# Retention attention into a low-rank mixer: half chunks of q and k loaded as rows of four tokens, k scaled in place of v in batch 0, one column tile for U^T x, and V loaded first as 32 rows

## The chip, the core and the metric

The kernel runs as one program on one core of a Trainium2 chip. The metric is the device time of one execution in microseconds (us); smaller is better. Five runs of the kernel before the change are known, and one further execution was profiled.

## What is computed

```python
def _attn_ref(q, k, v):                       # q, k, v: 8 x 8 x 576 x 64, float32
    scores = scale * np.matmul(q, k.transpose(0, 1, 3, 2))
    gamma = 1.0 - 2.0 ** (-5.0 - np.arange(H))
    rel = pos[:, None] - pos[None, :]
    Dmat = np.where(rel >= 0, gamma[:, None, None] ** rel[None], 0.0)
    return np.matmul(scores * Dmat[None], v)

def _moe_ref(x, U, V, w_ch1, w_ch2):          # x: 8 x 576 x 512
    xt = x.transpose(0, 2, 1)
    h = xt @ U @ V                            # U: 576 x 32, V: 32 x 576
    u = x + h.transpose(0, 2, 1)
    ch = np.maximum(u @ w_ch1, 0.0) @ w_ch2   # 512 x 2048, 2048 x 512
    return u + ch
```

The heads' outputs of a batch, side by side, are x. A decay factor gamma^(i-j) is split into a factor of the query's position and a factor of the key's position, so that a scaling of rows does the decay.

## The kernel before

**Tiles.** A batch has 576 tokens, four chunks of 128 and a half chunk of 64. Batches go in pairs: chunks 0 to 3 belong to the even batch, 5 to 8 to the odd one, and chunk 4 (`XC`) holds the last 64 tokens of the even batch in partitions 0 to 63 and the first 64 tokens of the odd batch in partitions 64 to 127. `kA qA vA` are the half-chunk loads of batch 0, `kB qB vB` those of batch 1.

**Per chunk.** q, k and v come in as float32, are cast to bfloat16 (`qkv`), and q and k are transposed (`qkT`). TensorE makes the scores of a chunk (`SC`), VectorE masks them (`ret`), TensorE multiplies them by v (`RV`) and adds q times the running state (`QS`); the state is the sum of k^T v over earlier chunks (`ST`). The result x of a batch is multiplied by U (`MA`, into `a_sb`, 32 rows of results for a part of the tokens), and `a_sb` by V gives h; u = x + h.

**Mixer.** Tokens are taken in groups of four chunks (g = 0 to 8). A group runs 16 blocks of Y1 (u @ w1, Relu on ScalarE) and four rows of Y2 (y @ w2), 864 ns of TensorE work each piece. The first group needs batch 0 finished and the first weights; from then on TensorE has mixer work to run, and the attention of later batches is put between it.

**Batches 0 and 1** are loaded differently from the rest. q comes in rows of four tokens (`load_q4`, 1-KB rows), k and v in rows of two tokens (`load_pair`, 512-byte rows); the half chunks come token by token (`load(..., early=True)`, 256-byte rows into 64 partitions). In `load_pair` the argument `scaled` says which of k (1) and v (2) is multiplied by the key's decay factor `vs2`: that one is a TENSOR_TENSOR on POOL (or DVE), the other a plain cast on ACT (or POOL or DVE).

**Order.** A planner (`Plan`) gives every operation a duration, a priority and dependencies, and writes out one static order for each engine. All loads go through SP's queue; their order in batches 0 and 1 is the list `line`. DMA durations in the plan are constants in the code. While TensorE has nothing to do before the first Y1, the program puts multiplications by zero there (`zeros`, rows `ps_big_t<-zer`).

**Where the change falls.** In the first 24 us: setup of constants (`consts_a`: L275 to L322), the casts of q (L378) and its evictions (L416, L419), casts of k and v (L521, L523), scalings (L526), transposes of k (L566) and evictions (L575, L577), masks (L713, L857), x (L757, L759, L932), `MA` and `a_sb` (L962), the copy of V (L1173, L1177), the first u transposed (`build`, L1041 and L1043), the first w1 casts (L1197), and Y1. All matmuls that are not transposes have line L326. V is loaded by one DMA that repeats its 32 rows four times, 128 partitions in all, since the four chunks' terms of `MA` land in four column tiles of 32 rows.

## Time and profile before

| | us |
|---|---|
| five runs, median | 338.34 |
| five runs, lowest and highest | 336.23, 339.85 |
| the profiled execution, its own time | 336.47 |
| its span, first to last instruction | 334.3 |
| first Y1 matmul starts (from the span's start) | 24.31 |
| last DVE addition starts | 330.41 |

| engine | busy us | share of the span |
|---|---|---|
| PE (TensorE matmul) | 325.6 | 97% |
| PEld (weight load, beside PE) | 160.8 | 48% |
| DVE (VectorE) | 150.3 | 45% |
| ACT (ScalarE) | 134.9 | 40% |
| POOL (GpSimd) | 84.9 | 25% |

All times of the profile are counted from the start of the span. In a line of the timeline the columns are start, duration, engine, source line, operation, output<-inputs, shapes, and how many instructions were merged; in brackets stands the idle time before it and what ended that. "SPq" lines are DMA issues by SP. The duration of a matmul includes its passage through the array, so consecutive matmuls overlap; a 128x512 one lasts 379 ns and its successor starts 216 ns after it. The granted TensorE clock was 0.998 of full speed.

### The profile page before, as it was taken

Reading aid. Unit: us, or ns where it says so; the run is one execution under the profiler, and the core shown is the slowest. Engines: PE = TensorE matmul, PEld = TensorE weight load, DVE = VectorE, ACT = ScalarE, POOL = GpSimd, SP = SyncE. Lnnn points to the kernel's source line nnn. Section 1 sums busy time; section 2 is a strip of 40 time slices with the busy share of each in tenths; the row PEclk is TensorE's granted clock in tenths of the full one; section 3 lists DMA queues with packets and bytes.
Section 4 is the critical chain, followed back from the end, with each engine's and each line's share of the span. In section 5 each row is a group of like instructions: output and inputs, shape, how many; then the busy total and the mean of one; then the engine's idle time right before and its main releaser. Section 6 shows DMA issues by size and latency. Waiting matters only on the chain.

```text
span 334.3 us, 6464 instructions
## 1 busy us (share of the span) xinstructions
PE 325.6 (97%) x2656; PEld 160.8 (48%) x2656; DVE 150.3 (45%) x238; ACT 134.9 (40%) x240; POOL 84.9 (25%) x116
## 2 busy tenths in 40 slices
PE   8989989999999999999999999999999999999995
PEld 3554445555545544554454455444544444444442
DVE  5852275786654537654476538533633020020011
ACT  4656554478303550265114521364035206404600
POOL 7657446521331222131132112200100010010010
PEclk9999999999999999999999999999999999999999
DMA  8999999999999999999999989913110320011012
GB/s 238 228 286 377 296 248 299 274 231 182 194 248 214 232 182 209 229 238 198 192 241 221 193 178 227 225 35 49 63 65 16 71 89 31 0 65 63 0 52 75
DMA packets 145169, 56.44 MB, mean 169 GB/s; under 512 B 128244, under 2 KB 138484, under 8 KB 145140
## 3 DMA queue, kind: packets, MB, share of 16 engines
q1 hardware_dynamic: 142420, 47.12, 68.5%
q0 software_dynamic: 2720, 8.92, 7.7%
q8 instruction: 21, 0.34, 0.4%
q14 instruction: 8, 0.07, 0.1%
HBM read 37.14 MB, written 9.44 MB: 139 GB/s over the span
## 4 chain that ended last, share of the span: by engine, by line
PE 91%; DMA 5%; POOL 1%; DVE 1%; ACT 1%; SPq 0%; issue 0%; DVEq 0%
PE ps_big_t L326 77%; PE ps_s L326 5%; PE ps_o L326 5%; PE ps_sc L326 3%; DMA st_st<-in_k_dram 3%; DMA vst<-in_moe_V_dram 3%; PE ps_big_t L566 1%; PE ps_sc L401 1%; DVE ret_t L713 0%; SPq L1156 0%; ACT qkT_t L575 0%; POOL w_sb L1197 0%; DVE o_sb L1127 0%; POOL VV L1173 0%; POOL VV L1177 0%
## 5 line engine op out<-in xcount | busy, mean ns | idle before, releaser
L326 PE MATMUL ps_big_t<-uT_t,w_sb 128*128 128x512 bf16 x576 | 133.7, 379 | 0.5 <-POOL w_sb L1197 0.5
L326 PE MATMUL ps_big_t<-w_sb,y_t 128*128 128x512 bf16 x576 | 133.1, 379 | 0.0
L1060 ACT ACTIVATE y_t<-ps_big_t 128x512 bf16<-128x512 f32 x144 | 85.8, 597 | 93.9 <-PE ps_big_t L326 93.7
L326 PEld LDWEIGHTS <-w_sb 128*128 128x128 bf16 x576 | 53.9, 98 | 62.1 <-POOL w_sb L1197 1.0
L326 PEld LDWEIGHTS <-y_t 128*128 128x128 bf16 x576 | 53.7, 98 | 60.7 <-issue 0.5
L1127 DVE TENSOR_TENSOR o_sb<-ps_big_t,u_t 128x512 f32<-128x512 f32 x36 | 24.7, 690 | 87.7 <-PE ps_big_t L326 87.5
L1134 POOL DMA_DIRECT2D out_dram<-o_sb x34 | 19.4, 570 | 161.4 <-DVE o_sb L1127 161.2
L472 POOL TENSOR_TENSOR qkv_t<-st_st,vscale 128x512 bf16<-128x512 f32 (+1 forms) x28 | 29.4, 1050 | 57.5 <-DMA st_st<-in_v_dram 46.3
L857 DVE TENSOR_TENSOR ret_t<-ps_sc,tri 128x1024 bf16<-128x1024 f32 x24 | 29.3, 1221 | 20.0 <-PE ps_sc L326 19.8
L798 ACT ACTIVATE s_sb<-ps_s 128x512 bf16<-128x512 f32 x22 | 13.1, 596 | 56.5 <-PE ps_s L326 56.4
L923 DVE TENSOR_TENSOR x_t<-ps_o,qscale 128x512 bf16<-128x512 f32 x27 | 18.6, 689 | 16.2 <-PE ps_o L326 16.1
L991 DVE TENSOR_TENSOR u_t<-ps_s,x_t 128x512 bf16<-128x512 f32 x20 | 13.8, 690 | 21.2 <-PE ps_s L326 21.1
L326 PEld LDWEIGHTS <-qkT_t 64*128 64x128 bf16 (+3 forms) x612 | 15.4, 99 | 11.2 <-issue 8.2
L326 PEld LDWEIGHTS <-ret_t 128*128 128x128 bf16 (+2 forms) x384 | 12.7, 99 | 7.3 <-issue 1.3
L468 DVE CAST qkv_t<-st_st 128x512 bf16<-128x512 f32 x27 | 13.0, 482 | 3.4 <-DMA st_st<-in_k_dram 3.4
L468 DVE CAST qkv_t<-q_st 128x512 bf16<-128x512 f32 x27 | 13.4, 497 | 2.3 <-DMA q_st<-in_q_dram 2.2
L326 PE MATMUL ps_sc<-qkT_t 64*128 64x128 bf16 (+2 forms) x336 | 13.5, 215 | 0.5 <-DVE ret_t L857 0.4
L326 PE MATMUL ps_o<-qkv_t,ret_t 128*128 128x64 bf16 (+2 forms) x344 | 13.2, 193 | 0.0
L326 PE MATMUL ps_s<-qkv_t 64*64 64x64 bf16 (+3 forms) x200 | 12.4, 207 | 0.3 <-ACT s_sb L675 0.3
L326 PEld LDWEIGHTS <-qkv_t 64*64 64x64 bf16 (+3 forms) x232 | 9.7, 104 | 6.1 <-issue 2.6
L991 DVE TENSOR_TENSOR u_t<-ps_o,x_t 128x512 bf16<-128x512 f32 x16 | 10.9, 684 | 3.4 <-PE ps_o L326 3.3
L575 ACT ACTIVATE qkT_t<-ps_big_t 128x512 bf16<-128x512 bf16 (+1 forms) x21 | 10.9, 555 | 2.0 <-PE ps_big_t L566 1.7
(101 smaller groups left out, 178.6 us busy)
## 6 DMA issues: line engine op xcount, KB each, us to landing
out_dram<-o_sb POOLq DMA_DIRECT2D x34, 256.0 KB, 3.2
st_st<-in_k_dram SPq DMA_DIRECT2D x24, 256.0 KB, 4.8
q_st<-in_q_dram SPq DMA_DIRECT2D x24, 256.0 KB, 4.5
st_st<-in_v_dram SPq DMA_DIRECT2D x24, 256.0 KB, 4.9
y_t<-in_moe_w_ch_dram SPq DMA_DIRECT2D x10, 512.0 KB, 9.9
wst_t<-in_moe_w_ch_dram SPq DMA_DIRECT2D x6, 512.0 KB, 7.5
st_st<-in_k_dram SPq DMA_DIRECT2D x4, 512.0 KB, 8.5
st_st<-in_v_dram SPq DMA_DIRECT2D x4, 512.0 KB, 7.8
```

The costliest lines, as they stand in the source:

```text
L326: nc.tensor.matmul(*a, skip_group_check=True, **kw)
L401: tps[a].append(nc.tensor.transpose(pst[:, hp // 2, r, hp % 2, :], t[:, 0, 2 * hp:2 * hp + 2, :].rearrange("p h d -> p (h d)"), ident,))
L468: nc.vector.tensor_copy(**args)
L472: eng.tensor_tensor(out=qkv[slot(*qk)][rows, 2, :, :], in0=at(2)[rows], in1=vscale[rows, c, :, None].to_broadcast([rows.stop - rows.start, ...
L575: nc.scalar.activation(func=AF.Copy, **args)
L798: nc.scalar.activation(out=s_sb[slot(*sk)], in_=ps_s.rearrange("p (a b) -> p a b", b=P), func=AF.Copy)
L857: nc.vector.tensor_tensor(out=ret[slot(*rk)][rows, hl, :, 0:n], in0=bank(hl.start)[rows, None, :, 0:n] if apart else ps_sc[rows, hl, :, 0: ...
L923: nc.vector.tensor_tensor(out=xs[slot(*xk)][rows].rearrange("p hp hl d -> p hl hp d"), in0=po[rows, :, 0:NHP * D].rearrange("p hl (hp d) - ...
L991: nc.vector.tensor_tensor(out=us[slot(*uk)].rearrange("p (hp hl d) -> p hp hl d", hl=2, d=D), in0=bank().rearrange("p (hp hl d) -> p hp hl ...
L1060: nc.scalar.activation(out=y1s[slot(*yk)][:, f, :], in_=ps_big[slot(*bk)], func=AF.Relu)
L1127: nc.vector.tensor_tensor(out=osb[slot(*ok)], in0=ps_big[slot(*bk)], in1=osb[slot(*ok)] if n else us[slot(*uk)], op=ALU.add)
L1134: eng.dma_start(out=out_flat[row:row + P, :], in_=osb[slot(*ok)])
```

## The change

It does these things. (1) `kA`, `qA` and `qB` are loaded in rows of four tokens of one head, 1 KB, 128 partitions by 256 values; `xqs` holds the decay factors for this layout (they need two POOL iotas, two selects and some DVE and ACT operations in `consts_a`); a new `t_x` sorts and transposes them by eight 64x64 matmuls against columns of the identity in place of four transposes. (2) In batch 0 both chunk pairs scale k and cast v (`scaled=1`). (3) The terms of `MA` of batch 0 all go to column tile 0 and add up there; `a_sb[0]` is zeroed in the setup and only 32 rows of it are written. (4) V comes first as 32 rows, VV is zeroed whole in the setup; the other 96 rows come late (`lv2`), then all 128 rows are cast by POOL (`Vr`) and copied (`V2`). (5) The order of loads, some planned durations (`DMA_LAT` 1700 to 2100 among them) and the place of `XC`'s transposes and scores in the plan are others, and the planner writes out another order for all engines.

```diff
-    DMA_LAT = 1700.0
+    DMA_LAT = 2100.0
...
+        nc.gpsimd.iota(xsel[:, 1, :], pattern=[[-HALF, H]], base=0, channel_multiplier=0, ...)
+        for b in range(2):
+            nc.gpsimd.iota(xqs[:, b, :], pattern=[[1, 4]], base=HALF if b else 4 * P, channel_multiplier=4, ...)
         for h in range(H):
             nc.vector.memset(lngt[:, :, h], lng[h])
+        nc.vector.tensor_copy(out=xsel[:, 0, :], in_=lngt[:, 0, :])
+        nc.vector.tensor_tensor(out=xsel[:, 1, :], in0=xsel[:, 1, :], in1=lngt[:, 0, :], op=ALU.mult)
...
-        nc.vector.memset(VV[:, S:S + HALF], 0.0)
+        for m, base in ((1, 0), (-1, 15)):
+            nc.gpsimd.affine_select(out=xsel, in_=xsel, pattern=[[0, 2], [-16 * m, H]], compare_op=ALU.is_ge,
+                                    fill=0.0, base=base, channel_multiplier=m)
+        nc.vector.tensor_reduce(out=xln, in_=xsel, axis=mybir.AxisListType.X, op=ALU.add)
+        nc.scalar.activation(out=xqs, in_=xqs, func=AF.Exp, bias=xln[:, 1:2], scale=xln[:, 0:1])
+        nc.vector.memset(VV, 0.0)
+        nc.vector.memset(a_sb[0], 0.0)
...
+    def t_x(j, b, prio):
...
+        def fn(e):
+            for r in range(4):
+                for hl in range(2):
+                    mm(pst()[HALF * hl:HALF * hl + HALF, r, :], xflat(j, b)[:, D * r:D * r + D],
+                       ident.rearrange("p (hp hl a) -> p hp hl a", hl=2, a=16)[:, :, hl, :], start=True, stop=True)
+        o = pl.op("PE", 300.0, fn, [st["kq"[j < 1], kb], ld["id"]], prio, acq=[bk])
+        def ev(e):
+            args = dict(
+                out=qkT[slot("qkT", (0, XC))][:, j * NHP:(j + 1) * NHP, rows].rearrange("p h (a r) -> p r h a", r=4),
+                in_=pst().rearrange("p r (h a) -> p r h a", a=16))
...
+        def four(j):
+            return b is not None and j == 0 or b == 0 and j == 1
...
+                if four(j):
+                    _, bb, t0 = pts[0]
+                    sent.append(nc.sync.dma_start(
+                        out=flat(j), in_=dram[bb, :, t0:t0 + HALF, :].rearrange("h (a r) d -> h a (r d)", r=4)))
+                    return
...
+            if four(0):
+                eng.tensor_tensor(
+                    out=xflat(0, b).rearrange("p (r d) -> p r d", d=D),
+                    in0=flat(0).rearrange("p (r d) -> p r d", d=D),
+                    in1=xqs[:, b, :, None].to_broadcast([P, 4, D]), op=ALU.mult)
...
-        terms = [(UU[:, 6 * par + i, :], c0 + i, 32 * i, every) for i in range(4)]
+        one = p == 0 and par == 0
+        terms = [(UU[:, 6 * par + i, :], c0 + i, 0 if one else 32 * i, every) for i in range(4)]
...
-            out=a_sb[par], in_=bank(), func=AF.Copy), [o], prio, acq=[(f"a{par}", p)], rel=[pak])
+            out=a_sb[par][0:R] if one else a_sb[par], in_=bank()[0:R] if one else bank(), func=AF.Copy), ...)
...
-            nc.sync.dma_start(out=vst, in_=moe_V[None, :, :].to_broadcast([4, R, S]))
+            nc.sync.dma_start(out=vst[0:R, :], in_=moe_V)
...
+        ld["lv2"] = DMA(500.0, 700.0, lambda e: nc.sync.dma_start(
+            out=vst[R:P, :], in_=moe_V[None, :, :].to_broadcast([3, R, S])), prio=-999.0)
...
+        ld["V"] = pl.op("ACT", 680.0, vcast(slice(0, R)), [ld["lv"]], -935.0,
+                        alt=[("DVE", 600.0), ("POOL", 700.0)])
+        ld["Vr"] = pl.op("POOL", 700.0, vcast(slice(0, P)), [ld["lv2"], ld["V"]], -150.0)
         ld["V2"] = pl.op("POOL", 600.0, lambda e: gp.tensor_copy(
-            out=VV[:, S + HALF:NV], in_=VV[:, 0:S]), [ld["V"]], -150.0)
+            out=VV[:, S + HALF:NV], in_=VV[:, 0:S]), [ld["Vr"]], -149.0)
...
-            load_pair(0, i, base + 20 * i, scaled=(2, 2)[i])
+            load_pair(0, i, base + 20 * i, scaled=1)
...
-    line = [...("k0 k2 v0 kA qA v2 vA lu lv w0 w1" + " " + "w2 w3 w4 w5 w6 w7 w8 w9 q4 w10 w11 kB k5 qB vB v5 k7 w12 w13 w14 w15 lub v7").split()]
+    line = [...("kA k0 k2 v0 qA vA v2 lu lv w0 w1" + " " + "w2 w3 w4 w5 w6 q4 w7 w8 w9 w10 w11 k5 kB qB vB v5 k7 w12 w13 lub w14 w15 v7 lv2").split()]
```

## The prediction

> **What bounds the kernel now.** I read the page first, then TensorE's busy time by stages, the chain of waits, and the timeline of the first 25 us.
>
> ```profile
> PE 325.6 (97%) x2656; PEld 160.8 (48%) x2656; DVE 150.3 (45%) x238; ACT 134.9 (40%) x240; POOL 84.9 (25%) x116
> ```
>
> TensorE is the bound. The stages (start:end, span, then busy us of each engine, at the end clock, DMA share and GB/s) say where it is not:
>
> ```profile
> 16.00:22.00 6.00, 5.56 (x138) 4.24 (x138) 2.42 (x5) 3.39 (x7) 2.34 (x4) 1.00 1.01 230
> 22.00:24.30 2.30, 1.24 (x5) 0.38 (x4) 1.01 (x2) 1.19 (x2) 2.20 (x4) 1.00 1.05 385
> 24.30:38.00 13.70, 13.69 (x64) 6.23 (x65) 2.86 (x5) 8.14 (x14) 9.36 (x9) 1.00 1.06 373
> 38.00:50.00 12.00, 11.06 (x102) 5.65 (x101) 8.44 (x15) 6.11 (x13) 5.74 (x6) 1.00 1.09 236
> 50.00:66.00 16.00, 15.19 (x255) 9.24 (x255) 10.65 (x14) 7.36 (x13) 10.37 (x13) 1.00 1.08 284
> 66.00:330.00 264.00, 264.00 (x1897) 127.47 (x1895) 112.68 (x170) 99.25 (x171) 43.97 (x57) 1.00 0.71 143
> ```
>
> From 66 to 330 us TensorE never idles, so nothing there can gain. What can move is the start of Y1 at 24.31 (before it TensorE partly multiplies zeros, so "busy" says little) and 0.94 + 0.81 = 1.75 us of idling between 38 and 66, where batch 1 is worked in. The timeline says what Y1 waits for:
>
> ```profile
> 21.17 0.60 ACT L962 ACTIVATE a_sb<-ps_big_t 128x512 bf16<-128x512 f32 x1 [0.46 <-PE ps_big_t L326]
> 21.87 0.67 POOL L1173 CAST VV<-vst 128x576 bf16<-128x576 f32 x1 [2.69 <-DMA vst<-in_moe_V_dram]
> 22.59 0.59 PE L326 MATMUL ps_big_t<-VV,a_sb 128*128 128x512 bf16 x2 [0.74 <-POOL VV L1173]
> 23.21 2.12 POOL L1197 CAST w_sb<-wst_t 128x1024 bf16<-128x1024 f32 x2
> 23.29 0.69 DVE L1043 CAST uT_t<-ps_big_t 128x512 bf16<-128x512 f32 x1 [3.33 <-PE ps_big_t L326]
> 24.31 2.76 PE L326 MATMUL ps_big_t<-uT_t,w_sb 128*128 128x512 bf16 x12 [0.48 <-POOL w_sb L1197]
> ```
>
> `a_sb` is done at 21.77, but V arrives late and costs TensorE 22.59 - 21.82 = 0.77 us; POOL then copies V a second time, so the first w1 cast ends at 24.25 instead of before uT at 23.98, another 0.28. Two lines of the chain show the load, and the first row above its price: 6 us at 230 GB/s, against 385 just after, with DMA fully busy in both.
>
> ```profile
> 13.39 8.43 DMA vst<-in_moe_V_dram
> 42.25 8.52 DMA st_st<-in_k_dram
> ```
>
> **The change, part by part, against the profiled 336.47 us** (span 334.3, 2.2 around it; the median, 338.34, lies 1.87 higher, and I carry differences over).
>
> *V in 32 rows.* 72 KB go in place of 288, the weights follow without the slow stretch, and the second copy leaves the place ahead of w1. V is then wanted only at a_sb's end: -0.77 and -0.28, -1.05 in all if a_sb comes at 21.77. Does it?
>
> *The setup.* These rows set when q's casts start:
>
> ```profile
> 2.65 0.09 DVE L311 MEMSET VV<- 128x32 uint32 x1
> 3.01 0.27 DVE L313 MEMSET sx<- 128x256 uint32 x1
> 3.08 0.87 POOL L318 TENSOR_SCALAR_AFFINE_SELECT tri<-tri 64x256 bf16<-64x256 bf16 x2
> 4.78 3.08 POOL L378 TENSOR_TENSOR qkv_t<-q_st,qs 128x256 bf16<-128x256 f32 x4 [0.84 <-DMA q_st<-in_q_dram]
> ```
>
> Zeroing 608 words of VV instead of 32 costs DVE 0.46 (a line through 0.09 for 32 and 0.27 for 256), a_sb 0.27, and the small operations for `xqs`, one of which waits for POOL's new iota, some 0.9. tri's memset stands behind all these, so it ends at 4.64 and not 3.01, POOL's two selects at 5.55, and POOL's four q casts start at 5.6, not 4.78: +0.8, no longer hidden behind the q load. (The program also puts ACT's 1.28 us table load behind a DVE operation; it ends near 4.3, under cover of 5.25, when DVE is through.)
>
> *k scaled.* POOL: casts to 8.7, kA (half of a 0.61 cast) to 9.0, then k0's two tokens by multiplication, 1.04 each; one row where DVE multiplied at the same time took 1.55, and DVE now does (its evictions end at 10.5), so 11.5. Before, POOL and ACT cast them side by side by 9.28. The first mask goes from 10.62 to 11.5 + 0.85 = 12.35, +1.7. Four masks follow at 1.21, the third ends at 15.98, and RV of the first pair, which reuses its bank, goes from 14.98 to 16.3. What is won at the other end: v2 needs only a plain cast (0.61) behind its arrival, where scaling ended at 16.92. Its arrival was 15.3 (POOL's 0.50 wait for it ended there); I keep 15.3 to 16.0, so 15.9 to 16.6. TensorE gets there at 17.2. From there, in its order: the states 0.75, scores of the half chunk 0.12, the first U term 0.35: RV of the second pair at 18.4, before 18.04.
>
> *One column tile.* Before, four U terms in four column tiles took 0.32 until the next instruction; now each takes 0.216 alone. One runs ahead of RV, three between transposes that must run anyway: +0.5 of work, of which about 0.4 fits in the 0.35 and 0.19 gaps in which TensorE waited for x. I take +0.12. So a_sb ends at 21.77 + 0.36 + 0.12 = 22.25, V's product starts at 22.3, Y1 (1.44 later, 22.59 to 24.03) at 23.74: **-0.57**. Bounds: -1.4 if POOL's multiplications don't slow each other and the setup hides; +0.8 if the U cast, now wanted at 17.7 (it ran at 18.88, POOL being busy until then), holds TensorE, with RV, both later products and MA queued behind it.
>
> *1-KB rows.* In the DMA view, 256-byte rows ran at 228 GB/s (window 10 to 12 us), 1-KB rows at 353 (4 to 6 us): 128 KB in 0.57 and 0.37 us, so -0.2 each for kA and qA, 0 if the rows don't matter. kA now stands ahead of k0, so k0, first cast at 7.98 before, is 0.37 to 0.57 later, near 8.5, and POOL is free for it only at 9.0: no term on the path. Were POOL free, k0's delay would count in full.
>
> The Trainium skill, "DMA: Bandwidth & Descriptors", section "Why a DMA increments its semaphore by 16 and not by 1", says a DMA uses the largest number of engines up to 16 that divides the slowest dimension of both its sides. That speaks against this part: kA and qA have 8 heads outermost, so 8 engines each, and the 96 spare rows of V a 3. It agrees with V's 4 copies crawling at 230 GB/s, though no view here counts engines. By it kA would gain nothing (0.7 us on half the engines, an estimate) and the spare rows would crawl as long as V did; the sum above stays, since POOL is later than k0 either way.
>
> *Later.* From 16 to 22 us DMA moved 1.38 MB where 385 GB/s moves 2.3: 2.4 us lost, plus 0.6 for the 216 KB that wait: weights, k and v of batch 1 come about 3 us earlier, TensorE 0.57. Of the 1.75 us idle, what hangs on loads (the second line of the chain above, k landing at 50.77, idles TensorE 0.5) goes; waits for masks and evictions stay: **-0.5**, bounds -1.75 and +1, the order being another. qB's four extra matmuls and the rest: +0.1. The spare rows of V: 0, hidden as long as they land before 64; the copy is wanted at 65.77.
>
> Sum: -0.57 - 0.5 + 0.1 = -0.97: 335.5 in a profiled execution, 337.4 on the median. A measurement of this kernel tells about 1% (3.4 us) from no change; this is 0.3%.
>
> **The rivals.**
>
> *Everything arrives early.* Setup hides, Y1 starts at 22.9 (-1.4), and batch 1's idling goes whole (-1.75): 338.34 - 3.1 = 335.2. For it: DMA 24 to 38 us runs at 373 GB/s, so a lead is kept. Against it: the masks in batch 1 (1.2 us each on DVE) stay.
>
> *The setup and the scaled k eat the gain.* POOL is on the path from 5.6 to 12.5; if each multiplication takes 1.55 and the U cast is late too, Y1 starts at 24.9 and batch 1 gains nothing: +0.6, 338.9. For it: the 1.55 row; against: TensorE then has only real work left and fewer zeros to push.
>
> *The spare rows of V collide with batch 2 (the other side).* They follow v7, whose scaling waited until 58.3, and batch 2's k and q queue behind.
>
> ```profile
> 58.32 1.04 POOL L526 TENSOR_TENSOR qkv_t<-st_st,vs 128x512 bf16<-128x512 f32 x1 [0.57 <-DMA st_st<-in_v_dram]
> 63.58 0.52 DVE L468 CAST qkv_t<-q_st 128x512 bf16<-128x512 f32 x1
> 65.77 0.71 PE L326 MATMUL ps_sc<-VV,a_sb 128*128 128x128 bf16 x4
> ```
>
> With 3 us of lead, v7 lands at 55.3; if the rows then take V's 8.43, they land at 63.7, two casts put V's copy at 65.1, and q of batch 2's second chunk (63.5 before) comes at 63.5 - 3 + 8.4 = 68.9. Its cast stands on DVE ahead of uT's eviction, so Y1 of group 1 goes from 67.3 to about 71.5: +4.2 - 0.5, 342.0. It decides once the rows land later than about 64; against it, 5 us or less after v7 costs nothing.
>
> **How the numbers follow.** Forecast 0.60, early arrivals 0.12, gain eaten 0.19, collision 0.09. The likeliest is 337.4; the range takes in the eaten gain and most of the early case, with run medians moving some 0.5: 335.0 to 339.6. Faster by over 1% (below 335.0) needs the best of the early case: 0.10. Slower by over 1% (above 341.7) needs the collision: 0.08. Within 1%: 0.82.
>
> **What would show it.** V's product starts right behind a_sb, Y1 at 23.2 to 24.3; POOL's first q cast near 5.6; first mask near 12.3; no wait of TensorE for VV or w1 before Y1; 66 to 330 us still full. I am wrong if Y1 starts before 22.8 or after 24.8, or TensorE idles over 3 us between 38 and 75.

## The result, and the profile after

The changed kernel took 340.97 us (median of 23 runs, 337.83 to 342.74). The kernel before, run beside it, took 338.1 (median of 42 runs: 41 from 336.1 to 342.6 and one at 420.2). Runs over 1.5% above the fastest of their kernel, such as that one, count as a slower state of the chip and are left out of the ratios. The ratio is 1.0072, with a 95% interval of 1.0048 to 1.0096: slower by 0.7%, where 0.3% faster was forecast. That is still within the 1% that the prediction called no change, but the time lies outside its range of 335.0 to 339.6. The profiled execution took 340.39, with a span of 338.6, 4.3 us more than before.

On the page, the busy times of the engines are much as they were; nothing here says where 4.3 us went:

```profile
PE 328.3 (97%) x2664; PEld 160.5 (47%) x2664; DVE 151.0 (45%) x242; ACT 135.8 (40%) x241; POOL 85.1 (25%) x122
```

TensorE's busy time by stages does (the same stages as the prediction's; the last three columns are clock, DMA share and GB/s):

```profile
16.00:22.00 6.00, 5.84 (x188) 4.49 (x188) 4.50 (x6) 4.21 (x8) 3.79 (x6) 1.00 0.77 221
38.00:50.00 12.00, 10.11 (x90) 4.93 (x87) 4.18 (x9) 6.71 (x15) 5.71 (x7) 1.00 1.16 256
50.00:66.00 16.00, 15.68 (x251) 8.67 (x250) 11.04 (x15) 6.38 (x11) 10.77 (x14) 1.00 0.94 243
66.00:330.00 264.00, 263.06 (x1903) 127.07 (x1904) 112.00 (x171) 101.20 (x174) 44.78 (x58) 1.00 0.74 144
```

The first row is the one to look at. V no longer crawls there, and yet DMA moved 221 GB/s, no more than before's 230. What changed is the share: 0.77 where before had 1.01, so some of the 16 engines had nothing to do for part of the time. This row alone doesn't say why: a second profile of the same kernel has 0.89 at 253 GB/s there, and a profile with all loads on 16 engines but one engine late from the start (c1 again, below) has 0.77 as well. TensorE's busy time, the first number behind the span of a stage, says that 38 to 50 us idles TensorE 1.89 us (before: 0.94), and 66 to 330 us 0.94 (before: 0). With Y1, which starts 1.65 later, the idling from 24.3 us on (2.22 + 0.94, against 1.76) makes 3.05 of the 4.3. The other 1.25 stands in no wait that a view shows.

The timeline of the changed kernel, with the rows that answer to the prediction's:

```profile
10.27 3.49 POOL L594 TENSOR_TENSOR qkv_t<-st_st,vs 128x512 bf16<-128x512 f32 x3 [0.83 <-DMA st_st<-in_k_dram]
13.22 1.23 DVE L781 TENSOR_TENSOR ret_t<-ps_o,tri 128x1024 bf16<-128x1024 f32 x1 [0.36 <-PE ps_o L342]
18.38 0.61 POOL L591 CAST qkv_t<-st_st 128x512 bf16<-128x512 f32 x1 [0.60 <-DMA st_st<-in_v_dram]
24.23 0.59 ACT L1031 ACTIVATE a_sb<-ps_big_t 32x512 bf16<-32x512 f32 x1 [1.34 <-PE ps_big_t L342]
24.87 0.61 PE L342 MATMUL ps_big_t<-VV,a_sb 128*128 128x512 bf16 x2
25.96 1.39 PE L342 MATMUL ps_big_t<-uT_t,w_sb 128*128 128x512 bf16 x5
45.03 0.63 ACT L589 ACTIVATE qkv_t<-st_st 128x512 bf16<-128x512 f32 x1 [2.66 <-DMA st_st<-in_k_dram]
61.30 0.66 POOL L1250 CAST VV<-vst 128x576 bf16<-128x576 f32 x1 [1.69 <-DMA vst<-in_moe_V_dram]
62.63 0.86 POOL L1255 COPY VV<-VV 128x576 bf16<-128x576 bf16 x1
```

POOL waited 0.83 us for k0, which the prediction had left off the path. V's product follows `a_sb` at once, as forecast, but `a_sb` itself ends at 24.82. At 45.03 ACT gets k of batch 1 after 2.66 us of waiting for its load; the view of the waits puts the price on TensorE first in its list:

```profile
PE ps_big_t L634 <- ACT qkv_t L589: 1.4, 1, 1.4
```

The chain of work that ended last goes through loads of k too (start, us):

```profile
3.16 8.78 DMA st_st<-in_k_dram
...
32.47 13.94 DMA st_st<-in_k_dram
```

The first is k2, k of batch 0's second chunk pair, which lands at 11.94; the second is kB, the half chunk of batch 1 that is queued right behind k5 and lands at 46.40. Before, V's load stood in the chain with 8.43 and k7 with 8.52: the chains pass through different loads, so these durations are not to be compared one by one. k5 itself was issued at 31.67 and landed at 45.01. In the kernel before it landed at 45.07, and its transposes started at 45.79, after TensorE had stood for 0.53; here they start at 45.72, after 1.39. So against the kernel before k5 is no later: TensorE, although its Y1 began 1.65 later, is ready for k5 some 0.9 us sooner, since its new order asks for it at an earlier point of the work. What k5 could have been shows in e8.

**When each load lands, engine by engine.** The trace holds the semaphore updates of SP's queue. A load of q or k in the kernel before counts 16 updates, all from its data; V's load, in 4 copies, one at issue and 4 later. kA and qA of the changed kernel count one at issue and 8 later, so each sits on 8 of the 16 engines, twice the bytes apiece; the 96 spare rows of V count 3 later ones. The Trainium skill says so ("DMA: Bandwidth & Descriptors", section "Why a DMA increments its semaphore by 16 and not by 1"): the engines used are the largest number up to 16 that divides the slowest dimension of both sides, and the rest of the 16 is written at once. The updates agree. Landing of the last engine, us; `after_again` and `before_again` are second profiles, and in e8 kA and qA are put on 16 engines (below):

| load | before | before_again | after | after_again | e8 |
|---|---|---|---|---|---|
| q, second piece | 6.12 | 6.23 | 7.42 | 6.32 | 6.39 |
| kA (half chunk) | 12.57 | 15.50 | 8.55 | 7.50 | 6.79 |
| k0, pair 0 | 7.93 | 9.56 | 10.13 | 9.13 | 8.57 |
| v0 | 11.70 | 14.60 | 14.67 | 13.56 | 12.43 |
| v2 | 15.30 | 17.78 | 18.33 | 17.70 | 15.76 |
| w0 | 22.91 | 24.89 | 21.34 | 20.49 | 18.87 |
| k5 (batch 1) | 45.07 | 46.48 | 45.01 | 44.29 | 41.02 |

In after_again, k0 landed on its first engine at 7.98 and on its last at 9.13, and v2 on the first at 15.40 and on the last at 17.70: half of the engines, as many as carry kA and qA, are late with what is behind them. (In `after` and `before_again` some engines were another 1 to 4 us late from the loads of k on; that spread of the start is no part of the change, for before_again has it too.)

### The profile page after: what moved, and what is told of

It is laid out like the page before. It is cut to its first block, busy times and chain, and to the rows that moved or that the text cites. A ratio compares the mean times of both kernels' runs of the same rounds, so it can differ in the third digit from the quotient of the medians.

```text
span 338.6 us, 6487 instructions
## 1 busy us (share of the span) xinstructions
PE 328.3 (97%) x2664; PEld 160.5 (47%) x2664; DVE 151.0 (45%) x242; ACT 135.8 (40%) x241; POOL 85.1 (25%) x122
## 4 chain that ended last, share of the span: by engine, by line
PE 78%; DMA 15%; SPq 3%; DVE 2%; issue 1%; ACT 1%; POOL 0%; DVEq 0%; ACTq 0%
PE ps_big_t L342 66%; DMA st_st<-in_k_dram 11%; PE ps_o L342 4%; PE ps_s L342 4%; PE ps_sc L342 3%; DMA q_st<-in_q_dram 3%; DMA wst_t<-in_moe_w_ch_dram 1%; PE ps_big_t L634 1%; DVE u_t L1060 1%; SPq L1233 1%; SPq L1225 0%; DVE o_sb L1196 0%; SPq L510 0%; DVE qkv_t L530 0%; DVE ret_t L925 0%
## 5 line engine op out<-in xcount | busy, mean ns | idle before, releaser
L1196 DVE TENSOR_TENSOR o_sb<-ps_big_t,u_t 128x512 f32<-128x512 f32 x36 | 24.8, 690 | 91.8 <-PE ps_big_t L342 90.4
L530 DVE CAST qkv_t<-q_st 128x512 bf16<-128x512 f32 x27 | 11.4, 423 | 9.1 <-DMA q_st<-in_q_dram 8.9
L342 PEld LDWEIGHTS <-qkv_t 128*128 128x128 bf16 (+3 forms) x256 | 10.1, 105 | 7.2 <-issue 2.5
```

Source lines behind the costliest of these rows:

```text
L342: nc.tensor.matmul(*a, skip_group_check=True, **kw)
L530: nc.vector.tensor_copy(**args)
L1196: nc.vector.tensor_tensor(out=osb[slot(*ok)], in0=ps_big[slot(*bk)], in1=osb[slot(*ok)] if n else us[slot(*uk)], op=ALU.add)
```

## The experiments

Unless another is named, each kernel is the changed one with the edit shown. Four sets were run, each beside its own runs of the kernel before: after_again with e1, e2 and e3; e4 to e7; before_again with e8, c1 and c2; e9, c3 and c1_again. Ratios are against the kernel before of the same set, with 95% intervals.

**The changed kernel again**, unedited, for a second profile.

> The changed kernel once more, for a second profile. If the half chunk's k, now third in SP's queue, is what delays the first loads, the second half of q lands near 7.4 us and the first pair of k near 10.1 us again (5.3 and 10.1 in the first profile, against 4.6, 6.1 and 7.9 before), and Y1 starts near 26.0. If the late landings were chance, they come near 6.2 and 8.7 here, the first mask near 12.0 and Y1 near 24.8.

341.81 us, 1.0080 [1.0051, 1.0109]. The first mask came at 12.22 and not 13.22, Y1 at 25.34, and the span was longer all the same, 341.1:

```profile
16.00:22.00 6.00, 5.58 (x173) 4.28 (x170) 3.76 (x6) 3.78 (x8) 3.49 (x6) 1.00 0.89 253
38.00:50.00 12.00, 10.21 (x96) 4.96 (x94) 4.87 (x10) 6.87 (x15) 5.37 (x6) 1.00 1.13 240
```

So 1 us at the first mask is the start's spread, and the wait between 38 and 50 us belongs to the kernel. From 66 to 330 us TensorE idled 3.99, of which 2.27 around 148 to 151. DVE takes its instructions in order and stands 2.79 us before a cast of q whose load has not landed; the eviction that TensorE needs is behind it.

```profile
147.02 0.43 DVE L530 CAST qkv_t<-q_st 128x512 bf16<-128x512 f32 x1 [2.79 <-DMA q_st<-in_q_dram]
147.36 0.68 DVE L991 TENSOR_TENSOR x_t<-ps_o,qscale 128x512 bf16<-128x512 f32 x1
148.10 0.29 PE L342 MATMUL ps_o<-s_sb,qkT_t 64*128 64x64 bf16 x8 [1.22 <-DVE x_t L991]
```

TensorE's way to RV of both pairs, for the account below. In this order the sorting of the half chunk's q (15.73), the scores of the fourth chunk (15.97) and a product for the state (16.64) stand ahead of RV of pair 0; the only wait between the two RVs is for ACT's cast of v2:

```profile
15.73 0.32 PE L342 MATMUL ps_big_t<-ident,qkv_t 128*64 128x64 bf16 x8
15.97 0.42 PE L342 MATMUL ps_sc<-qkT_t 64*64 64x128 bf16 x16
...
16.64 0.44 PE L342 MATMUL ps_s<-qkv_t 128*64 128x64 bf16 x16
17.02 0.64 PE L342 MATMUL ps_o<-qkv_t,ret_t 64*128 64x64 bf16 x32
...
18.41 0.44 PE L342 MATMUL ps_s<-qkv_t 64*64 64x64 bf16 x16 [0.42 <-ACT qkv_t L589]
...
19.71 0.64 PE L342 MATMUL ps_o<-qkv_t,ret_t 64*128 64x64 bf16 x32
```

**The setup behind the q casts (e1).** The small operations for `xqs` and the zeroing of V and `a_sb` leave the head.

```diff
-        nc.vector.tensor_reduce(out=xln, in_=xsel, ...)       # and the selects, xqs's exp
-        nc.vector.memset(VV, 0.0)
-        nc.vector.memset(a_sb[0], 0.0)
+    def consts_c(): ...                                       # the same, put behind DVE's q evictions
+    put(consts_b, ...)                                        # POOL's selects: behind kA's cast
+    put(consts_c, ...)
```

> The scales of the half chunk and the two memsets (V's tile, a_sb) are computed behind q's scalings; nothing else moves. Theory set-up: q's scalings started at 5.47 instead of 4.71 and the rest of the start hangs on that, so the first mask comes 0.6 to 0.8 us earlier (12.5), Y1 near 25.2, the whole 0.6 us shorter than the changed kernel. Rival queue: the first pair of k lands at 10.1 whatever q's scalings do, the mask stays near 13.2 and the time within 0.2 us.

340.25 us, 1.0065 [1.0041, 1.0089]; after_again in the same set 1.0080. DVE's first q cast moved from 5.36 to 4.74, the first mask hardly:

```profile
4.74 1.18 DVE L398 TENSOR_TENSOR qkv_t<-q_st,qs 128x256 bf16<-128x256 f32 x2 [0.75 <-DMA q_st<-in_q_dram]
...
12.03 1.22 DVE L785 TENSOR_TENSOR ret_t<-ps_o,tri 128x1024 bf16<-128x1024 f32 x1 [0.31 <-PE ps_o L346]
```

k0 landed at 9.00. The setup's 0.6 us are real, and nearly all hidden: what follows waits for k0. Y1 came at 25.11 (after_again 25.34).

**kA behind v0 in SP's queue alone (e2).** One issue moved, all engines' orders kept.

```diff
+    moved = next(x for x in order if x[0] is load_op("kA"))
+    order.remove(moved)
+    order.insert(next(i for i, x in enumerate(order) if x[0] is load_op("v0")) + 1, moved)
```

> Only SP's order changes: the half chunk's k goes behind v of the first pair, as the kernel before had it. Theory queue: q's two halves land near 4.6 and 6.1, the first pair of k near 8.0 to 8.5 instead of 10.1; the first mask 1 us earlier or more (12.0), Y1 near 25.0, the whole 0.7 to 1.2 us shorter than the changed kernel. Rival set-up: q's scalings still start at 5.5, the first mask moves by 0.3 us at most. Rival of the later stages: the start gets shorter, and TensorE idles as much longer between 38 and 75 us, so that the time stays.

345.45 us, 1.0193 [1.0153, 1.0233]. k0 landed at 8.79, only 0.34 before after_again's, and that helped nobody: POOL's order still has kA's cast ahead of k0's scalings. The waits of TensorE, then POOL's timeline:

```profile
PE ps_big_t L342 <- POOL qkv_t L528: 4.3, 1, 4.3
```

```profile
12.95 0.40 POOL L528 CAST qkv_t<-st_st 128x256 bf16<-128x256 f32 x1 [4.15 <-DMA st_st<-in_k_dram]
13.31 3.04 POOL L594 TENSOR_TENSOR qkv_t<-st_st,vs 128x512 bf16<-128x512 f32 x3
```

It doesn't tell the theories apart, for the edit put in a wait of its own. What it does show: Y1 moved to 32.22, 6.9 us later than in after_again, and the time grew by 3.6 only. About half of this delay of Y1 was won back on the way. In the profiles TensorE idles 1.79 us less than in after_again between 38 and 50 (there is no wait for k5 left), 0.42 more from 50 to 66 and 3.6 less behind 66; what wins it back was not separated.

**V in 32 rows and one column tile, alone (e3).** The kernel before, with these two parts and nothing of k and q.

```diff
-            nc.sync.dma_start(out=vst, in_=moe_V[None, :, :].to_broadcast([4, R, S]))
+            nc.sync.dma_start(out=vst[0:R, :], in_=moe_V)
...
-        terms = [(UU[:, 6 * par + i, :], c0 + i, 32 * i, every) for i in range(4)]
+        terms = [(UU[:, 6 * par + i, :], c0 + i, 0 if one else 32 * i, every) for i in range(4)]
...
+    line = [...("... w12 w13 w14 w15 lub v7 lv2")...]         # the spare rows behind v7
```

> The kernel before with one part of the change alone: V early in 32 rows, its 96 spare rows last in the line, batch 0's U^T x in one column tile. If this part brings what was forecast for it, V's product follows the eviction of a_sb with no wait (0.9 us less), Y1 starts near 23.5 and the whole is 0.7 to 1.0 us shorter than before. If the spare rows cost batch 2 its loads, TensorE idles over 2 us between 62 and 80 and the time is as before or up to 1 us longer.

340.39 us, 1.0059 [1.0032, 1.0085]: slower, with Y1 at 23.30, 1.0 us *earlier* than before. The 16 to 22 us row moved 320 GB/s instead of 230, so the crawl is gone. Then TensorE's busy time in steps of 2 us, and one row of its timeline:

```profile
50.00:52.00 2.00, 1.11 (x51) 0.91 (x44) 1.48 (x2) 1.87 (x4) 1.04 (x1) 1.00 1.04 372
52.00:54.00 2.00, 1.01 (x17) 0.91 (x17) 0.19 (x1) 0.00 (x0) 1.04 (x1) 0.57 1.09 297
54.00:56.00 2.00, 2.00 (x23) 0.98 (x22) 1.48 (x2) 0.60 (x1) 1.30 (x2) 0.50 1.03 220
56.00:58.00 2.00, 2.00 (x6) 0.73 (x5) 1.12 (x2) 0.00 (x0) 0.81 (x1) 0.50 0.78 158
58.00:60.00 2.00, 2.00 (x8) 0.73 (x7) 0.78 (x1) 0.00 (x0) 0.90 (x2) 0.72 0.33 77
```

```profile
52.99 0.45 PE L327 MATMUL ps_o<-qkv_t,ret_t 64*128 64x64 bf16 x10 [1.14 <-issue]
```

TensorE comes to batch 1 earlier, idles near half of 50 to 54 us, once 1.14 us with no releaser that the profile shows (it says "issue"), in the middle of 32 like matmuls, and its clock is then granted at half: by the rows at 0.57 and 0.72, from 52.3 to 59.1. The clock column costs up to 0.43 x 2 + 0.5 x 2 + 0.5 x 2 + 0.28 x 2 = 3.4 us, more than Y1 gained. The mean granted clock of the kernel's seven runs was 0.988 to 0.995, that of all runs of before beside them 0.995 to 1.000, so the profiled execution was hardly alone in it. The Trainium skill describes such a gate ("TensorE: Matmul & The Clock Gate", section "What's actually happening"): the clock is halved after an idle window of about 3.4 us and comes back after as long a busy one. The rows agree with the halving, but not with an idle window: the longest gap was 1.14 us, TensorE was idle for 1.88 of 4 us in three gaps, and the half clock lasted 6.8, though TensorE was busy for the last 6 of them.

**kA back behind v0, with all orders made anew (e4).** The list that the planner starts from, so that POOL's order changes with SP's.

```diff
-    line = [...] + [load_op(x) for x in ("kA k0 k2 v0 qA vA v2 lu lv w0 w1" + ...
+    line = [...] + [load_op(x) for x in ("k0 k2 v0 kA qA vA v2 lu lv w0 w1" + ...
```

> The half chunk's k goes behind v of the first pair, and the order of all engines is planned anew for it, so that no engine is left waiting for it (in e2 POOL was). Theory queue: the first pair of k lands near 8.0 instead of 9.1, the first mask 1.0 to 1.2 us earlier than in the changed kernel (near 11.2), Y1 near 24.5; if the start is what was lost, the time falls by 0.7 to 1.0 us, to about 1.005 of before. Theory later stages: Y1 is earlier by as much, but TensorE waits as much more for the loads of batch 1 (38 to 75 us) and from 140 to 220, and the time stays within 0.4 us of the changed kernel's.

339.13 us, 1.0011 [0.9977, 1.0046]: no loss is seen in this set, which had no runs of the changed kernel beside it. In its profile one engine was late from the start (15 had k0 by 7.93, the last at 9.55), so its first mask at 12.64 doesn't show what the move is worth there.

**k cast, v scaled, as before (e5).**

```diff
-            load_pair(0, i, base + 20 * i, scaled=1)
+            load_pair(0, i, base + 20 * i, scaled=2)
```

> Batch 0's v is scaled and its k only cast, as before. Theory: POOL's three scalings of k in a row (1.1 us each) set the four masks 1.2 to 1.6 us apart (1.13 before); with casts of 0.6 us on ACT and POOL the first mask comes 0.4 us and the fourth 0.8 to 1.2 us earlier, Y1 0.5 to 1.0 us earlier. Rival: the scaled v's go back to the end of POOL's chain (2 us of scalings before the half chunk's), the gain is lost at RV and Y1 moves by less than 0.3 us. Of the time, half of what Y1 gains at most, because batch 1's loads do not move.

340.66 us, 1.0037 [1.0007, 1.0067]. The four masks stand 1.14 apart again (in after 1.46, 1.14 and 1.61), and the fourth ends at 16.57:

```profile
11.95 1.23 DVE L781 TENSOR_TENSOR ret_t<-ps_o,tri 128x1024 bf16<-128x1024 f32 x1 [0.59 <-PE ps_o L342]
...
15.35 1.22 DVE L781 TENSOR_TENSOR ret_t<-ps_sc,tri 128x1024 bf16<-128x1024 f32 x1
17.24 0.69 DVE L594 TENSOR_TENSOR qkv_t<-st_st,vs 128x512 bf16<-128x512 f32 x1 [0.67 <-DMA st_st<-in_v_dram]
```

But the scaling is now behind v, and v is late: `a_sb` starts at 23.88, no earlier than after_again's 23.61. So k's scaling costs near 1 us at the masks; what is won there is lost again before `a_sb` (Y1 at 25.61).

**V in 128 rows again (e6)**, with four column tiles, the rest as changed.

```diff
-            nc.sync.dma_start(out=vst[0:R, :], in_=moe_V)
+            nc.sync.dma_start(out=vst, in_=moe_V[None, :, :].to_broadcast([4, R, S]))
...
-        one = p == 0 and par == 0
+        one = False
```

> V in one early load of 128 rows, U^T x in four column tiles, no spare rows late: that part of the change undone. If that part pays where the start is later by 2 us anyway, V's product waits for V again (0 to 0.7 us) but a_sb comes 0.4 to 0.9 us earlier because the four column tiles run together: Y1 within 0.5 us of 25.3. If the 96 spare rows are what makes batch 2 late, the idling of TensorE between 66 and 80 (0.5 to 1.4 us) goes away and the time falls by about 1 us.

341.9 us, 1.0084 [1.0052, 1.0116]. w0 landed at 23.00 instead of 20.49, so the crawl does cost the weights 2.5 us, but the time is as after's. That is not to say that V's 32 rows are worth nothing: here TensorE idled 1.09 us from 24.3 to 38 and 2.42 from 38 to 50, and its clock was granted at half from 48.5 to 51.9, behind gaps of 0.34, 0.32 and 1.17 us; the mean clock of seven of its eight runs was 0.993 to 0.995. Y1 came at 24.65, 0.7 ahead of after_again's, for TensorE waited for no v2 (landed at 16.92). From RV of pair 1 to `a_sb`'s start it took 3.89 with four column tiles, after_again 3.90 with one: in this order the column tile itself costs nothing; what costs is that the terms and the transposes between them now come behind the last `x_t`. In e3, with the order of before and one tile, it took 3.53, and before 3.13.

**The planner's assumed latency of a load at 1700 ns, as before (e7).**

```diff
-    DMA_LAT = 2100.0
+    DMA_LAT = 1700.0
```

> Only the planner's assumed latency of a transfer goes back from 2100 to 1700; the work is the same and only its order moves. Theory order: the stalls at 147 to 151 and near 215 us (0.3 to 2.7 us, none before) come from loads planned to be issued behind a run of transposes on SP, and the order planned with 1700 has them as before: TensorE idles under 0.3 us from 100 to 250, the time falls by 1 us or more. Rival: the stalls follow from the start and from batch 1 being late, and stay.

340.97 us, 1.0054 [1.0021, 1.0086]. Y1 moved to 27.63 (in this profile the clock was granted at half from 20.6 to 24.0), the waits at 147 us went. Another order loses its time in other places; the total doesn't tell it from the changed kernel.

**The kernel before again**, one profile.

> The kernel before once more, for a second profile. If its first profile (span 334.3) was a fortunate one, the span comes near 336 and TensorE idles 3 us or more between the start of Y1 and 250 us instead of 1.8; if the two stages are steady, Y1 starts near 24.3 and nothing idles after 66.

340.24 us, span 338.1, first mask at 11.89, `a_sb` starting at 24.08, Y1 at 26.26. In this execution one engine ran behind the other 15 from the first loads of k on, by 1.4 us at k0 (8.14 on the fifteenth, 9.56 on the last) and 2.8 at v0 (11.82 and 14.60). And TensorE idles here between 66 and 330 us too: 3.87 by the view, of which some is records that the trace lacks, but two waits have a releaser, 0.62 at 117.3 and, for the eviction of `x_t` that after_again waits for at 148,

```profile
146.90 0.29 PE L326 MATMUL ps_o<-s_sb,qkT_t 64*128 64x64 bf16 x8 [0.58 <-DVE x_t L923]
```

One profile of the same kernel and another therefore differ by 2 us at Y1 and 3.8 in the span; the profile that the prediction was built on, with nothing idle behind 66, was one of the good ones. Comparisons of single profiles below 2 us count for little in what follows, and landing times on the eighth engine for more than those on the last.

**kA and qA on all 16 engines (e8).** The rows' order in the tile is changed from head first to token group first: 16 groups outermost instead of 8 heads, the same 1-KB rows. The sorting matrix and the scales follow (two more operations in the setup).

```diff
-   out=flat(j), in_=dram[bb, :, t0:t0 + HALF, :].rearrange("h (a r) d -> h a (r d)", r=4)))
+   out=flat(j), in_=dram[bb, :, t0:t0 + HALF, :].rearrange("h (a r) d -> a h (r d)", r=4)))
...
-   ident.rearrange("p (hp hl a) -> p hp hl a", hl=2, a=16)[:, :, hl, :], start=True, stop=True)
+   ident.rearrange("p (a hp hl) -> p hp hl a", hl=2, a=16)[:, :, hl, :], start=True, stop=True)
```

> Only the row order of the half chunk changes: partition 8a + h instead of 16h + a, so that the slowest dimension of the source is 16 and not 8; the sorting matmuls and the scales follow. Theory engines: in the changed kernel the half chunk's k sits on 8 of the 16 DMA engines, 16 KB on each, and every later load lands 0.7 to 1.1 us later on those 8 (9 semaphore updates for the load, the first pair of k spread from 7.98 to 9.13). With 16 engines there are 16 updates, the first pair of k lands within 0.5 us, near 8.4, the first mask near 11.6 (12.2), Y1 0.4 to 0.7 us earlier than 25.3. Rival bytes: the first pair of k is late by the 128 KB ahead of it however they are spread (0.4 us at the rate of q's halves), or by the start-up of the queue; then it lands near 9.0 still. Time: 0.3 to 0.7 us less than the changed kernel.

339.86 us, 1.0027 [0.9997, 1.0058]. The updates of kA and qA are 16. kA landed at 6.79, k0 at 8.57 (0.64 after before's 7.93; the prediction had +0.37 to +0.57), v2 at 15.76 (the prediction kept 15.3 to 16.0), w0 at 18.87, k5 at 41.02: 3.3 us before after_again's. Busy time by stages:

```profile
16.00:22.00 6.00, 6.00 (x183) 4.47 (x178) 4.24 (x6) 3.94 (x9) 3.74 (x6) 1.00 1.03 361
...
38.00:50.00 12.00, 11.79 (x116) 5.89 (x116) 6.65 (x12) 7.79 (x16) 5.80 (x6) 1.00 1.06 267
...
100.00:150.00 50.00, 46.57 (x370) 23.05 (x376) 25.64 (x39) 17.79 (x31) 9.77 (x13) 1.00 1.17 206
```

361 GB/s at a share of 1.03, where after_again had 253 at 0.89, and the wait for k5 is gone: 0.21 us idle between 38 and 50 instead of 1.79. Y1 did not move (25.36), because the longer setup now held the q casts (DVE 6.00, POOL 6.70, first mask 12.99). And 3.4 us are missing between 100 and 150: 0.50 at 145.8 and 1.34 at 149.5 in waits of the kind shown at 147, 1.13 at 107.9 with no releaser, the rest in records that the trace lacks.

**16 engines, the setup's work moved too, kA behind v0 (c1), then with k cast (c2).**

```diff
-    line = [...("kA k0 k2 v0 qA ...")]
+    line = [...("k0 k2 v0 kA qA ...")]                        # with e8's edits
+    nc.scalar.activation(out=VV[:, a:b], in_=zer[:, 0:b - a], func=AF.Copy)   # zeroing on ACT, not DVE
+    def consts_b(): ...                                       # scales: on DVE behind its q casts
# c2 adds
+            load_pair(0, i, base + 20 * i, scaled=2)
```

> Three things together, k still scaled: the half chunk's k behind v of the first pair with the order planned anew, all 16 engines for its loads, and the scales and zeroed tiles moved into idle times of DVE and ACT. Theory start: q's scalings at 4.7, the first pair of k near 7.9, the first mask near 11.2, Y1 near 24.0, and a time at or under before (ratio 0.997 to 1.001). Rival later stages: Y1 comes as early, but batch 1's loads do not, TensorE waits between 43 and 50 us for them, ratio 1.001 to 1.005.

> As c1, with v scaled and k cast, as before. Theory: the four masks are 1.13 us apart again and the first is near 10.7, V is no longer waited for, so Y1 starts near 23.6, 0.7 us ahead of before; if nothing is lost later the time is 0.5 us under before (ratio 0.996 to 1.000). Rival later stages: as in e3, what is won at Y1 is idled away between 45 and 80 us, or TensorE's clock drops there; ratio 1.002 to 1.007.

c1: 338.43 us, 0.9979 [0.9943, 1.0015], first mask 11.16, Y1 24.72. c2: 339.34, 1.0004 [0.9975, 1.0033], first mask 10.68, Y1 25.02. Both intervals hold 1. In c1 a first mask that is 2.06 us earlier than after's gives only 1.24 at Y1: RV of pair 0 comes at 16.45, behind the half chunk's sorting (14.38), the fourth chunk's scores (15.40) and a product for the state (16.07), and behind it TensorE stands for 0.68 at 18.04 with no releaser.

**k alone on 16 engines (e9)**: e8's edit for kA, qA left on 8. If only the load ahead of the first k matters, this gives all of it back.

```diff
+   out=flat(j), in_=dram[bb, :, t0:t0 + HALF, :].rearrange(
+       "h (a r) d -> a h (r d)" if j == 1 else "h (a r) d -> h a (r d)", r=4)))
```

> The half chunk's k alone in the row order with 16 as the slowest dimension; its q (and that of batch 1) stays on 8 engines; set-up as in the changed kernel. Theory engines, adding up: each load of 128 KB on 8 engines holds those 8 engines 0.75 us longer, so the first pair of k lands near 8.5 (as in e8), but the first expert weights at 19.5 to 19.8, half way between e8's 18.87 and the changed kernel's 20.49. Y1 near 24.9, the time half way between e8 and the changed kernel (ratio 1.004 to 1.006). Rival: only the load ahead of the first pair of k matters, the weights land near 18.9 and the ratio is e8's or below (1.001 to 1.003).

339.01 us, 1.0049 [1.0026, 1.0072]. w0 landed at 18.58, k5 at 42.01, Y1 came at 24.65, TensorE idled 0.53 between 38 and 50 us. So the weights and k5 are nearly as early as e8's, though k0 (9.24) and v2 (16.58) are not: for what comes later, kA's half makes most of the delay. The time is not told from e8's or from after's.

**e8 with the setup moved (c3), and c1 a second time.**

```diff
# c3: e8 with c1's zeroing on ACT and its consts_b, kA still ahead of k0
```

> The changed kernel's order of all engines, with 16 engines for the half chunk's loads as in e8 and the scales and zeroed tiles moved into idle times. Theory: with the k no longer late the set-up is uncovered, so moving it now pays what it did not in e1: q's scalings at 4.75 (6.0 in e8), the first mask near 11.6, Y1 near 24.3, 1.0 us before e8's 25.36; ratio 0.998 to 1.001. Rival: POOL's three scalings of k set the masks in any case, Y1 near 25.0, ratio as e8's.

> c1 once more, for a second set of times and a second profile. If its gain over before is real, the ratio is 0.995 to 0.999 again; if it was the luck of one set of runs, it is 1.000 to 1.003.

c3: 339.41 us, 1.0039 [1.0009, 1.0070]; nothing idles between 38 and 50 us (12.00 of 12.00 busy), Y1 at 24.70, span 335.8. c1 again: 339.56, 1.0040 [1.0007, 1.0074], where its first set gave 0.9979. The same kernel in two sets, 0.6% apart: differences of this size between my versions are not resolved, and none was shown to beat the kernel before. In c1's second profile, as in e4's, one engine was late from the start; kA and qA are on 16 engines here, and yet the row of 16 to 22 us has after's share of 0.77, k5 lands at 43.94 instead of 41.09, and TensorE waits 0.3 for it:

```profile
16.00:22.00 6.00, 6.00 (x180) 4.39 (x176) 3.62 (x5) 4.46 (x9) 3.74 (x7) 1.00 0.77 229
```

## Why the prediction was wrong

The way to Y1, step by step (us; after_again stands beside after because its start was as undisturbed as before's):

| step | before | predicted | after_again | after |
|---|---|---|---|---|
| first mask starts | 10.62 | 12.35 | 12.22 | 13.22 |
| third mask ends | 14.11 | 15.98 | 16.03 | 17.04 |
| RV of pair 0 | 14.98 | 16.3 | 17.02 | 18.00 |
| v2 has landed | 15.30 | 15.3 to 16.0 | 17.70 | 18.33 |
| RV of pair 1 | 18.04 | 18.4 | 19.71 | 20.34 |
| `a_sb` ends | 21.77 | 22.25 | 24.20 | 24.82 |
| V's product | 22.59 | 22.3 | 24.25 | 24.87 |
| Y1 | 24.31 | 23.74 | 25.34 | 25.96 |

**The first step that failed: the way from the third mask to Y1.** The masks came as forecast (third mask's end to 0.05 us), Y1 1.60 later than forecast in after_again. Four terms make the 1.60:

- RV of pair 0, 0.72 late (17.02 for 16.3). The prediction let RV follow the third mask ("RV of the first pair, which reuses its bank, goes from 14.98 to 16.3") and overlooked TensorE's own new order, which puts the sorting of the half chunk's q, the fourth chunk's scores and a state product ahead of it. The same order gives 16.69 in e6, 16.82 in e9, 16.88 in c3; nowhere in it does TensorE stand still just before.
- From there to RV of pair 1, 0.59 more than forecast. 0.42 of it is a wait for v2. "1-KB rows" had quoted the rule on engines and set it aside ("the sum above stays, since POOL is later than k0 either way"): it looked only at the load next in line, k0, and there it was nearly right (POOL came to k0 at 9.27, k0 landed at 9.13). But loads on 8 engines also leave those engines behind for later loads: v2, kept at 15.3 to 16.0, came at 17.70, against 15.76, 16.03 and 16.23 with 16 engines in e8, c2 and c3. The price on TensorE is small, since TensorE was at v2 only at 17.99, where the prediction had it at 17.2: 0.42 here, 0.36 in e1, about 0.1 in after, nothing in e6.
- From RV of pair 1 to the end of `a_sb`, 0.64 more: the column tile, below.
- From V's product to Y1, 0.35 less (1.09 for 1.44).

So by these rows most of the delay is the new order of TensorE and not the loads: without any wait for v2, in e6, e9 and c3, RV of pair 1 comes at 19.02 to 19.08 and Y1 at 24.65 to 24.70, still 0.9 behind the forecast and some 0.35 behind the kernel before. These are single profiles that agree; no run gave TensorE its old order with the rest of the change, so this share is read from the rows and not shown by an edit.

**The second: "Later: -0.5".** Measured, TensorE idled 0.46 more than before from 24.3 to 66 in after, 0.35 more in after_again. The weights did come earlier than before (w0 20.49 for 22.91), by what V no longer takes; the loads on 8 engines took 0.2 to 1.6 us of that back (w0 at 18.87 in e8, 19.08 to 19.30 in e5 and e1). k5 landed at 44.29 and 45.01, before's at 45.07, so the lead of 3 us was not there; the new order asks for k5 sooner, and that cost 1.29 to 1.39 us. With 16 engines the lead was there (k5 at 41.02 in e8, 42.01 in e9, 41.69 in c3), no wait for k5 was left, and the idling from 38 to 66 was 0.79, 0.84 and 0.31 against before's 1.75: the term came true, and more, once the loads were spread. That loads on 16 engines take the wait away is shown; a shorter time is not. e8's interval overlaps after's, e9 and c3 stay above 1 with kA on 16 engines and no wait for k5, e4 stands in another set, and c1 in two sets differs by 0.6%.

**One column tile, mis-sized.** +0.12 was taken, of a bound of +0.5. From RV of pair 1 to `a_sb`'s start, before took 3.13, after_again 3.90: +0.77. With the order of before the tile costs +0.40 (e3: 3.53); in the new order the order alone makes the +0.77, for e6 with four tiles has 3.89. The gaps in which "about 0.4 fits" are gone: neither e3 nor after_again has a gap over 0.1 us there.

**What held.** First mask and third mask, to 0.13 and 0.05 us. The setup: POOL's first q cast came at 5.85 in after and 6.06 in after_again (5.6 forecast), and was covered, by the late k0 (e1). V in 32 rows: V's product stands directly behind `a_sb`, no wait for VV or w1 before Y1, and from V's product to Y1 it is 1.09 instead of 1.72; in e3 Y1 gained the 1.0 us that the part was priced at (-1.05), in part by luck: V's wait went as priced (0.76 for 0.77), but the stretch from V's product to Y1 shrank by 0.63 where 0.28 was priced, and `a_sb` came 0.39 later where 0.12 was. Only, a gain at Y1 was not a gain in the end: e3 lost it in 50 to 59 us, in a half clock that no term of the sum had. The spare rows: cast at 61.30 and copied by 63.49, ahead of 64, so their rival did not decide.

**The rivals.** "The setup and the scaled k eat the gain" (338.9, Y1 24.9) came nearest in time and place, by another mechanism: not POOL's multiplications, which took 3.49 for three (1.16 each, between the rows of 1.04 and 1.55), but TensorE's order and the late v2. "Early arrivals" needed the 3 us lead that was there only with 16 engines. The signs named for being wrong were right: Y1 after 24.8, and TensorE idle for 3.46 us between 38 and 75 in after_again (2.82 in after; the sign was 3).

**What stays open.** "66 to 330 us still full" failed: after lost 0.94 there, after_again 3.99 (2.27 of it at 148 to 151), e8 3.4 between 100 and 150; e3, with the order of before, lost nothing between 100 and 150. But the kernel before has such waits too in its second profile, so that nothing idled there in the first may have been luck, and how much of these losses is the change's is not known. The casts that wait in DVE's order for late loads are seen, why the new orders make them late was not separated from the change itself (e7's other order had none at 147 and was no faster). Nor is the 1.25 us of span explained that no wait shows. So the 0.7% as a whole is not traced to one cause: what is shown is the later Y1, with its four terms, and the wait for k5.

## What to carry to other kernels

Price a load not by when it lands but by the engines it uses: count its semaphore updates, and where they are fewer than 16, charge the skew to every load queued behind it, not only to its own reader; if a reordering of the outermost dimension gives 16, the loads come earlier (here k5 by 3.3 us), though no shorter time was shown for it. Where a change brings a new order of an engine, read that order between the operations of the sum: here, by the rows, it cost more at Y1 than the loads did. A forecast that adds differences stage by stage must also ask whether a gain survives the next bound: here 1 us won at Y1 was lost again in batch 1, and half of a 7 us delay (e2) cost nothing. And look at a second profile of the same kernel before trusting a figure under 2 us.

## What the runs showed of the hardware that I had not expected

- Two loads of 128 KB on 8 engines (kA and qA) skew the queue behind them: k0, behind kA, spread over 7.98 to 9.13, v2, behind both, over 15.40 to 17.70 (after_again). With both on 16 engines the same loads spread 8.10 to 8.57 and 15.18 to 15.76 (e8).
- Short waits of TensorE can be followed by a loss larger than themselves: in e3 three gaps of 0.31, 0.43 and 1.14 us were followed by 6.8 us at half the granted clock (52.3 to 59.1); in e6, gaps of 0.34, 0.32 and 1.17 by 3.4 us of it (48.5 to 51.9).
- In some executions (before_again, e4, c1_again) a single engine is 1 to 3 us behind the other 15 from the first loads of k on; in before_again the first mask came 1.3 us later than in the other profile of the same kernel.
- TensorE stood 1.14 us in e3, 1.7 in e2 and 1.13 in e8 with no releaser that the profile names. What held it was not separated by any run.
